# Wider pieces for the weight conversion, and the other head first in the products with v

## The chip, the cores and the metric

One core of one Trainium2 chip runs one program. The metric is device time in microseconds (us), from one execution to the next the same work; the profile that is read below is one more execution of the same program, taken with the hardware profiler. PE is TensorE, PEld its weight loads, DVE VectorE, ACT ScalarE, POOL GpSimd, SP the queue that issues the DMAs.

## The reference

Three blocks follow each other, for 4 batches of 576 tokens:

```python
# attention: 8 heads of 64, the 32 largest scores of each row are kept
scores = scale * (q @ k^T); mask = scores >= 32nd largest of the row
attn = softmax(scores where mask); x = attn @ v          # (4, 576, 512)
# gate: causal convolution over 5 tokens, two 512x512 products
x = (sigmoid(conv(x)) * (x @ w_val)) @ w_out
# phase mixer
theta = x @ w_theta
y = w_tok_r @ (x * cos(theta)) + w_tok_i @ (x * sin(theta))
u = x + y; out = u + max(u @ w_ch, 0)
```

The weights of the last two blocks arrive as float64 and have to be made float32 on the chip: `w_val`, `w_out`, `w_theta`, `w_ch` are 512x512, `w_tok` stands as 1152 rows of 576, `conv` as 512 rows of 5.

## The kernel before, in words

**Steps.** The attention works on 144 tiles of 128 rows of scores (576 wide), about one tile a step. Two heads (j = 0 and 1) of one pair share a part: a part's tiles are listed with head 0 first and head 1 last (lines 144 to 152). In step i several tiles are in flight: scores of tile i+3 on PE (`scores_pe`, line 530), their eviction on ACT, the largest values of tile i on DVE (`pick`, lines 581 to 587), a sign count on ACT (line 594), a product on POOL (`below`, lines 602 and 603), the threshold on DVE (`rest`, line 608), the exponential on ACT, the mask on DVE (`mask`, line 661), the transposes on PE (`turn`, line 674) and their eviction to `pT` on ACT (`turn_out`, line 693). The order of these stages in a step is the list `SOON`, in the second half of the steps `STEP` (lines 58 to 60, loop at line 1348). Lines 71 and 124 hold the engines DVE and ACT to the order in which the program is written; the order of PE, POOL and SP is chosen when the program is built, by what is ready.

**The end of a part.** When a part's last tile has been turned, `close` (line 708) issues the product with v, `px` (lines 760 to 766): for each of 5 blocks of keys one product for head 0, into partitions 0 to 63, and one for head 1, into partitions 64 to 127. There are 32 such groups, of 256 or 320 columns. Each product is two records in the profile, so a group has 20.

**Jobs.** The gate and the mixer of a batch are `front` and `back` (lines 840 and 1086): generators whose products are cut into portions that `work` (line 1224) puts into the steps, some 4150 ns of PE work a step (`BASE`), in the order of the batches. A job that meets something not yet written yields "sync" and tries again in the next step. `back` first waits until every weight is converted (`while any(lacking.values())`, line 1101).

**The conversion.** `weights` (line 358) cuts the six weights into pieces of 128 rows and `half` = 256 columns, 54 in all: 52 with 256 numbers a partition, one with 64 and one with 20. `convert` (line 1302) begins `PIECES` = 1 piece a step, and each piece moves on one stage a step through `cvt` (line 305):

1. a DMA brings the 64-bit words into one of six raw buffers (`RAWS`, line 53; line 318);
2. a step of waiting (`WAIT`), then on ACT the absolute value of the high words into one of two `tmp` buffers (line 329) and the shifted low words (line 330);
3. three DVE operations are put on the list `fill` (lines 337, 338 and 333): two of one input on `tmp`, one of two inputs;
4. `mask_between` (line 1275) takes three from `fill` in a step: the first, then the mask of line 661, then the second and third;
5. POOL adds the two words into the weight (line 351) and, for `w_theta`, ACT scales it (line 355); then `lacking` falls by one.

The raw and `tmp` buffers stand in memory that later holds the split halves of weight blocks (`hi0` to `hi3`, `lo0` to `lo3`, `place`, line 441). `want` (line 453) asks for the halves of block m of a weight as soon as the block before it is out (lines 867, 896, 1098 and 1148).

Of the kernel before, what the change touches and what calls it, by code (L numbers as in the profile page):

```python
# [12 lines left out]
F32R = mybir.dt.float32r  # L13
# [36 lines left out]
PARTS = (1, 1)  # L50
DRAIN = 5000.0
VAT = (11, 12)
RAWS = ("hi0", "hi1", "hi2", "hi3", "lo2", "lo3")
WAIT = 1
PIECES = lambda i: 1.0

LEAST = 2.0 ** -15 * 1.125
STEP = ['close', 'rest', 'below', 'pick', 'nmax', 'select', 'mask', 'check', 'expo', 'mid', 'chains', 'turn_out', 'convert', 'turn', 'scores_out', 'later', 'count', 'work_1', 'scores_pe', 'work_2', 'loads', 'chains']
# [32 lines left out]
def mixer(ctx, tc, qT, kT, vt, w_val, conv_t, w_out, w_theta, w_tok, w_ch, out, flag):  # L91
# [213 lines left out]
    def cvt(name, dst, words, factor, c):  # L305


        p0, a, w = dst.shape
        n = a * w
        r, k = c % len(W["raw"]), c % len(W["tmp"])  # L310
        while r in taken:
            yield None
        taken.add(r)
        raw = W["raw"][r][:p0, :n]
        t = W["tmp"][k][:p0, :n]
        lo, hi = raw[:, :, 0], raw[:, :, 1]
        def bring_in():
            ins = nc.sync.dma_start(raw.rearrange("p (a w) t -> p a w t", a=a), words).ins
            if c < len(RAWS):
                tc.add_manual_dep(ins, evicted[0].name, mybir.DependencyInfo(  # L320
                    mybir.DependencyClass.Sync, mybir.DependencyReason.SCHED_ONLY), reason="behind the heads")
            if loaded[0] is not None:
                tc.add_manual_dep(ins, loaded[0].name, mybir.DependencyInfo(
                    mybir.DependencyClass.NoSync, mybir.DependencyReason.SCHED_ONLY), reason="heads go first")

        yield bring_in

        def on_act():
            nc.scalar.activation(t, hi.bitcast(F32), AF.Abs)
            nc.scalar.activation(lo, lo.bitcast(U32), AF.Copy, scale=2.0 ** -29)  # L330

        def joined():
            nc.vector.scalar_tensor_tensor(hi, hi, -0x40000000, t.bitcast(I32), ALU.bitwise_and, ALU.bitwise_or)
            taken.remove(("tmp", k))

        def on_dve():
            fill.append(lambda: nc.vector.tensor_scalar(t, t, LEAST, None, ALU.max))
            fill.append(lambda: nc.vector.tensor_scalar(
                t.bitcast(I32), t.bitcast(I32), 3, 0x3FFFFFF8, ALU.logical_shift_left, ALU.bitwise_and))
            fill.append(joined)  # L340

        for _ in range(WAIT):
            yield None
        while ("tmp", k) in taken:
            yield None
        taken.add(("tmp", k))
        yield on_act
        yield on_dve
        while ("tmp", k) in taken:
            yield None  # L350
        yield lambda: nc.gpsimd.tensor_tensor(dst.bitcast(I32), *(h.rearrange("p (a w) -> p a w", a=a) for h in (hi, lo)),
                                                ALU.add)
        taken.remove(r)
        if factor is not None:
            yield lambda: nc.scalar.activation(dst, dst, AF.Copy, scale=factor)
        lacking[name] -= 1

    def weights():
        half = DM // 2
        W["raw"] = [ml.tile([P, half, 2], I32, tag=t, name=f"raw_{t}") for t in RAWS]  # L360
        W["tmp"] = [ml.tile([P, half], F32, tag=f"lo{x}", name=f"tmp{x}") for x in range(2)]
        pieces = []
        for name, src, factor in (("conv", conv_t, None), ("val", w_val, None), ("out", w_out, None),
                                  ("theta", w_theta, 1.0 / (2.0 * math.pi)), ("tok", w_tok, None), ("ch", w_ch, None)):
            rows, n = src.shape
            W[name] = cp.tile([P, -(-rows // P), n], F32, tag=f"w_{name}", name=f"w_{name}")
            words = src.bitcast(I32).rearrange("r (n t) -> r n t", t=2)

            chunks = -(-rows // P)
            cuts = [(c, 1, o, o + half) for c in range(chunks) for o in range(0, n - half + 1, half)]  # L370
            cuts += [(c, min(4, chunks - c), n // half * half, n) for c in range(0, chunks, 4) if n % half]
            for c, a, o, e in cuts:
                src = words[c * P : (c + a) * P, o:e].rearrange("(a p) n t -> p a n t", a=a)
                lacking[name] = lacking.get(name, 0) + 1
                pieces.append((name, W[name][:, c : c + a, o:e], src, factor, len(pieces)))
        return pieces
# [64 lines left out]
    def place(k, m):  # L441

        if k < 3 or k % 3 == 2:
            return [ml.tile([P, DM], F32R if k < 3 else I32, tag=f"{t}{m}", name=f"{t}{m}_{k}") for t in ("hi", "lo")]
        if (k, 0) not in places:
            names = ("val", "out") if k % 3 == 0 else ("theta", "ch")
            for t in range(2):
                places[k, t] = cp.tile([P, NC, DM], I32, tag=f"w_{names[t]}", name=f"w{t}_{k}")
        return [places[k, t][:, m, :] for t in range(2)]
# [3 lines left out]
    def want(b, name, last=NC - 1):  # L453

        k = PHASES.index((b, name)) if b else -1
        if k > 2:
            return
        for m in range(last + 1):
            if (b, name, m) in mats:
                continue  # L460
            src = W[name][:, m, :] if name == "theta" else W[name][:, :, m * P : (m + 1) * P]
            both = place(k, m)
            mats[b, name, m] = both
            stored[name, m] = dp.tile([P, 2, DM], I32, name=f"{name}{m}")

            def store(both=both, to=stored[name, m]):
                for t in range(2):
                    nc.sync.dma_start(to[:, t, :], both[t].bitcast(I32))

            hi, lo = (t if name == "theta" else t.rearrange("p (c w) -> p c w", c=NC) for t in both)  # L470
            halve(hi, lo, src, ("w", b, name, m), store)
# [236 lines left out]
    def close(part):  # L708
# [50 lines left out]
        owed[0] -= 8.3 * w  # L759
        px = ps_m.tile([P, w], F32, tag="m", name=f"px_{u}_{x}")  # L760
        for c in range(NF + 1):
            for j in range(2):
                d = slice(64 * j, 64 * j + 64)
                of_v, k = (v[:, c, d], j * NF + c) if c < NF else (v_last[:, d], 2 * NF)
                nc.tensor.matmul(px[d, :], of_v, pT[:, k, :],  # L765
                                 start=(c == 0), stop=(c == NF), skip_group_check=True)
# [73 lines left out]
    def front(b, xs):  # L840
# [13 lines left out]
        def val_out(m, x, ps):  # L854
            lo, hi = COLS[x]

            def f():
                g = gv[m][:, lo:hi]
                nc.vector.scalar_tensor_tensor(g, g, 1.0, ps, ALU.add, ALU.mult)
                if not three:  # L860
                    done.add(("G", b, m, x))
                    return
                if m == NC - 1:
                    for c in range(NC):
                        halve(*chunk(b, x, "G", c), gv[c][:, lo:hi], ("G", b, c, x))
                if x:
                    want(b, "out", m)
            return f

# [20 lines left out]
        def x2_out(m, x, ps):  # L890
            lo, hi = COLS[x]

            def f():
                nc.scalar.activation(x2T[:, m, lo:hi], ps, AF.Copy, scale=0.5)
                if three and x:
                    want(b, "theta", m)
                if three and m == NC - 1:
                    halve_room(b, x, "L", x2T)
                done.add(("x2", b, m, x))
            return f  # L900
# [185 lines left out]
    def back(b):  # L1086
        x2T = ms.pop(b)

        def y_out(m, h, ps):
            lo, hi = COLS[h]  # L1090

            def f():
                nc.vector.tensor_tensor(x2T[:, m, lo:hi], ps, x2T[:, m, lo:hi], ALU.add)
                if m == NC - 1 and (h or b == B - 1):
                    for k in (h,) if b == B - 1 else range(2):
                        halve_room(b, k, "U", x2T)
                if not h:
                    want(b, "ch", m)
            return f

# [40 lines left out]
        def h_out(m, h, ps):  # L1141
            lo, hi = COLS[h]

            def f():
                nc.vector.scalar_tensor_tensor(x2T[:, m, lo:hi], ps, 0.0, x2T[:, m, lo:hi], ALU.max, ALU.add)
                n = b + 1
                if h and n in THREE:
                    want(n, "val", m)
                    if (n * NP + m, 0) in there:
                        split_x(n, m, 0)  # L1150
                done.add(("o", b, m, h))
            return f
# [121 lines left out]

    def mask_between(i):

        for x in range(3):
            if fill:
                fill.pop(0)()
            if x == 0:  # L1280
                inside(i, mask)
# [122 lines left out]
```

## Time and profile before

| | |
|---|---|
| median of 3 runs | 838.05 us (836.03 to 838.68) |
| the profiled execution's own time | 838.7 us |
| its span, first to last instruction | 836.9 us |
| PE busy | 734.5 us, 88% |
| DVE busy | 677.7 us, 81% |
| ACT busy | 639.4 us, 76% |
| POOL busy | 440.5 us, 53% |
| mean granted TensorE clock | 0.969 of full |

The attention's tiles and the jobs run side by side for some 700 us; after that only jobs are left. A busy share is a mean over stages with different limits, so the time is cut into windows first. The records of one engine overlap a little at their ends (the next instruction starts before the last has finished), so the cost of an operation on an engine that never idles is read from start to start.

### The profile page before, as it was taken

The page shows a single profiled execution, that of the slowest core. Times are in us where ns is not written, and L with a number is a line of the kernel's source. Part 1 is how long each engine was busy: PE and PEld are TensorE (multiplying, and loading weights), DVE is VectorE, ACT ScalarE, POOL GpSimd, SP SyncE. Part 2 cuts the span into 40 slices and gives each one's busy share as a digit, 9 for nine tenths or more (in the row PEclk, how much of TensorE's full clock was granted, in tenths as well). Part 3 has the DMA queues.
Part 4 walks back from the last instruction along what each step waited for, and adds up shares of the span by engine and source line. Part 5 has one row for each costly group of instructions (what it writes and reads, how often), then busy time and mean ns, then how long its engine had stood idle before and what let it go on. Part 6 is the DMA issues. An engine that isn't in the chain of part 4 may idle for free.

```text
span 836.9 us, 15761 instructions
## 1 busy us (share of the span) xinstructions
PE 734.5 (88%) x4478; PEld 584.1 (70%) x4478; DVE 677.7 (81%) x2786; ACT 639.4 (76%) x1573; POOL 440.5 (53%) x583
## 2 busy tenths in 40 slices
PE   4476889968899899898699989999989899999995
PEld 3244667535665676697587777778988767898895
DVE  6999999979987889999899879989998685353522
ACT  6678898889788777989789888889987785346511
POOL 5876665545643536557677735547796143004600
PEclk9999899979999899999899989999999999999998
DMA  5566666635440253437455543234753300070002
GB/s 167 147 159 194 165 171 168 179 94 129 119 108 15 47 156 82 101 93 224 112 179 168 151 138 84 45 84 112 193 166 119 101 1 15 1 231 28 2 1 61
DMA packets 73601, 94.35 MB, mean 113 GB/s; under 512 B 13728, under 2 KB 37152, under 8 KB 73504
## 3 DMA queue, kind: packets, MB, share of 16 engines
q1 hardware_dynamic: 73184, 92.82, 40.8%
q8 instruction: 38, 0.62, 0.3%
q10 hardware_dynamic: 320, 0.43, 0.2%
q14 instruction: 59, 0.48, 0.2%
HBM read 49.96 MB, written 13.11 MB: 75 GB/s over the span
## 4 chain that ended last, share of the span: by engine, by line
PE 39%; DVE 32%; ACT 13%; POOL 6%; issue 5%; DMA 4%; SPq 0%; ACTq 0%; POOLq 0%
PE py L1114 8%; DVE cand L581 7%; DVE thrs L608 5%; PE px L765 5%; DVE s L661 4%; PE pth L516 4%; PE ph L516 3%; PE px2t L516 3%; PE pval L516 3%; PE py L1133 3%; DVE cand L587 3%; DVE tops L585 3%; PE pt L674 3%; ACT n L594 2%; POOL y L602 2%
## 5 line engine op out<-in xcount | busy, mean ns | idle before, releaser
L602 POOL TENSOR_TENSOR y<-s,n 128x576 f32<-128x576 f32 x144 | 190.9, 1325 | 158.1 <-DVE thrs L608 116.0
L581 DVE MAX8 cand<-s 128x8 f32<-128x96 f32 x864 | 211.4, 245 | 1.0 <-ACT s L559 1.0
L661 DVE SCALAR_TENSOR_TENSOR s<-s,thrs,e 128x576 f32<-128x576 f32 x144 | 137.7, 956 | 9.7 <-ACT e L202 9.7
L594 ACT ACTIVATE n<-s,tops 128x576 bf16<-128x576 f32 x144 | 112.1, 779 | 40.3 <-POOL y L602 18.8
L559 ACT ACTIVATE s<-ps 128x256 f32<-128x256 f32 (+1 forms) x288 | 103.1, 406 | 26.2 <-PE ps L737 10.3
L1114 PE MATMUL py<-w_tok,z 128*128 128x256 f32 (+1 forms) x432 | 118.8, 416 | 1.7 <-DVE z L973 1.7
L674 PE MATMUL pt<-ident,s 128*128 128x128 f32 x576 | 95.3, 286 | 28.4 <-ACT pT L693 15.4
L608 DVE MAX8 thrs<-y 128x8 f32<-128x584 f32 x144 | 109.5, 760 | 8.3 <-POOL y L603 8.0
L202 ACT ACTIVATE e<-s,least 128x576 f32<-128x576 f32 x144 | 110.9, 770 | 0.5 <-DVE s L661 0.4
L674 PEld LDWEIGHTS pt<-ident,s 128*128 128x128 f32 x576 | 69.0, 145 | 56.5 <-ACT pT L693 25.9
L545 PE MATMUL ps<-kh_None,q 128*128 128x256 f32 x240 | 92.0, 390 | 5.2 <-ACT rb L744 2.5
L1114 PEld LDWEIGHTS py<-w_tok,z 128*128 128x128 f32 x432 | 79.6, 195 | 22.3 <-DVE z L973 2.5
L765 PE MATMUL px<-pT,v 128*64 128x256 f32 (+1 forms) x512 | 84.5, 431 | 10.1 <-ACT pT L693 10.1
L693 ACT COPY pT<-pt 128x512 f32<-128x512 f32 x128 | 73.2, 572 | 24.4 <-PE pt L674 13.4
L585 DVE MAX8 tops<-cand 128x8 f32<-128x48 f32 x432 | 83.3, 193 | 0.1
L546 PE MATMUL ps<-kl_None,q 128*128 128x256 f32 x240 | 71.5, 301 | 0.0
L765 PEld LDWEIGHTS px<-pT,v 128*64 128x64 f32 x512 | 37.1, 141 | 43.4 <-issue 12.5
L545 PEld LDWEIGHTS ps<-kh_None,q 128*128 128x128 f32 x240 | 46.7, 195 | 20.2 <-ACT s L559 8.3
L545 PE MATMUL ps<-kh,q 128*128 128x256 f32 (+1 forms) x80 | 35.7, 454 | 24.3 <-ACT s L559 11.0
L587 DVE MATCH_REPLACE8 cand<-tops,cand 128x48 f32<-128x48 f32 x288 | 55.5, 193 | 0.0
L546 PEld LDWEIGHTS ps<-kl_None,q 128*128 128x128 f32 x240 | 47.1, 196 | 2.3 <-issue 0.9
L682 ACT COPY pT<-ps 64x128 f32<-64x128 f32 (+1 forms) x160 | 39.4, 246 | 12.0 <-PE ps L678 5.6
(215 smaller groups left out, 1742.2 us busy)
## 6 DMA issues: line engine op xcount, KB each, us to landing
kh_None<-kh_None SPq DMA_DIRECT2D x48, 144.0 KB, 2.6
kl_None<-kl_None SPq DMA_DIRECT2D x48, 144.0 KB, 2.7
v<-in_vt_dram SPq DMA_DIRECT2D x20, 256.0 KB, 3.4
out_dram<-x2T SPq DMA_DIRECT2D x16, 256.0 KB, 3.4
w<-ch SPq DMA_DIRECT2D x16, 256.0 KB, 4.1
w<-theta SPq DMA_DIRECT2D x16, 256.0 KB, 5.6
raw_hi<-in_w_tok_dram SPq DMA_DIRECT2D x14, 256.0 KB, 4.1
kh<-kh SPq DMA_DIRECT2D x24, 144.0 KB, 2.5
```

What stands on the lines that cost most here:

```text
L202: ins = nc.scalar.activation(out, src, func, **more).ins
L516: nc.tensor.matmul(ps[o : o + n], x, y, start=(i + k == 0), stop=(i == last and k == len(ways) - 1), skip_group_check=(n < P))
L545: nc.tensor.matmul(bank[:, :w], q2, kh[:, lo:hi], start=(j == js[0]), stop=False)
L546: nc.tensor.matmul(bank[:, :w], q2, kl[:, lo:hi], start=False, stop=(j == js[-1]))
L581: nc.vector.max(d["cand"][:, k, 8 * x : 8 * x + 8], s_tiles[i][:, x * SUB : (x + 1) * SUB])
L594: nc.scalar.activation(n, s_tiles[i], AF.Sign, bias=d["tops"][:, k, KC - 1 : KC], scale=-(1.0 + 2.0 ** -22), accum_out=acc)
L602: nc.gpsimd.tensor_tensor(y[:, :S], s_tiles[i], d.pop(("n", k)), ALU.mult)
L608: nc.vector.max(thrs[:, N - 1 - i : N - 1 - i + NK], d.pop(("y", k)))
L661: nc.vector.scalar_tensor_tensor(p, p, thr(i), e.exp, ALU.is_ge, ALU.mult, accum_out=part["sums"][:, e.slot : e.slot + 1])
L674: nc.tensor.transpose(e.pt[:, c, :], p[:, c * P : (c + 1) * P], ident)
L765: nc.tensor.matmul(px[d, :], of_v, pT[:, k, :], start=(c == 0), stop=(c == NF), skip_group_check=True)
L1114: nc.tensor.matmul(ps, z[:, m * P : (m + 1) * P], W["tok"][:, w, lo:hi], start=(i + k == 0), stop=(i == NF))
```

## The change

Pieces are 512 columns wide, so there are 28: 26 with 512 numbers a partition (one of them 8 strips of 64 columns of `w_tok`), one with 64 and one with 20. One begins every other step. The raw buffers are three of double size, `tmp` two of double size. The second ACT operation (line 330) moves one step later, and two operations instead of three are taken from `fill` in a step, so that they fall: first, mask, second; in the next step: third, mask. The halves of weight blocks stand in pairs of blocks, and `want` asks for them two at a time. In `px` head 1's product goes before head 0's.

```diff
-RAWS = ("hi0", "hi1", "hi2", "hi3", "lo2", "lo3")
+RAWS = ("hi01", "hi23", "lo23")
 WAIT = 1
-PIECES = lambda i: 1.0
+PIECES = lambda i: 0.5
...
-        def on_act():
+        def size():
             nc.scalar.activation(t, hi.bitcast(F32), AF.Abs)
+
+        def tail():
             nc.scalar.activation(lo, lo.bitcast(U32), AF.Copy, scale=2.0 ** -29)
...
         def on_dve():
+            tail()
             fill.append(lambda: nc.vector.tensor_scalar(t, t, LEAST, None, ALU.max))
...
-        yield on_act
+        yield size
         yield on_dve
...
     def weights():
-        half = DM // 2
+        half = DM
...
-            cuts += [(c, min(4, chunks - c), n // half * half, n) for c in range(0, chunks, 4) if n % half]
+            cuts += [(c, min(8, chunks - c), n // half * half, n) for c in range(0, chunks, 8) if n % half]
...
     def place(k, m):
 
         if k < 3 or k % 3 == 2:
-            return [ml.tile([P, DM], F32R if k < 3 else I32, tag=f"{t}{m}", name=f"{t}{m}_{k}") for t in ("hi", "lo")]
+            dt = F32R if k < 3 else I32
+            both = []
+            for t in ("hi", "lo"):
+                if (t, m) in (("lo", 0), ("lo", 1)):
+                    both.append(ml.tile([P, DM], dt, tag=f"{t}{m}", name=f"{t}{m}_{k}"))
+                    continue
+                pair = f"{t}{m - m % 2}{m - m % 2 + 1}"
+                if (pair, k) not in places:
+                    places[pair, k] = ml.tile([P, 2, DM], dt, tag=pair, name=f"{pair}_{k}")
+                both.append(places[pair, k][:, m % 2, :])
+            return both
...
         for c in range(NF + 1):
-            for j in range(2):
+            for j in (1, 0):
                 d = slice(64 * j, 64 * j + 64)
...
-                if x:
+                if x and m % 2:
                     want(b, "out", m)
...
-                if three and x:
+                if three and x and m % 2:
                     want(b, "theta", m)
...
-                if not h:
+                if not h and m % 2:
                     want(b, "ch", m)
...
                 if h and n in THREE:
-                    want(n, "val", m)
+                    if m % 2:
+                        want(n, "val", m)
...
-        for x in range(3):
+        for x in range(2):
             if fill:
                 fill.pop(0)()
```

## Rows read from the trace of the kernel before

**Rows 1.** Windows: span, busy us of each engine (records), clock, DMA share, GB/s.
```profile
40.00:60.00 20.00, 14.90 (x57) 9.17 (x57) 19.86 (x93) 15.44 (x41) 14.09 (x20) 1.00 0.60 158
...
120.00:140.00 20.00, 19.61 (x112) 15.06 (x111) 19.86 (x93) 17.65 (x50) 12.84 (x18) 1.00 0.70 178
...
200.00:220.00 20.00, 16.06 (x87) 11.19 (x87) 19.86 (x93) 19.28 (x52) 12.51 (x17) 0.91 0.52 142
...
280.00:300.00 20.00, 20.00 (x111) 14.99 (x111) 17.79 (x76) 14.32 (x38) 8.85 (x11) 1.00 0.31 80
```

**Rows 2.** Timeline of DVE, 69.7 to 74 us: start, length, then the operation.
```profile
69.74 0.28 DVE L337 TENSOR_SCALAR tmp<-tmp 128x256 f32<-128x256 f32 x1
69.93 0.81 DVE L661 SCALAR_TENSOR_TENSOR s<-s,thrs,e 128x576 f32<-128x576 f32 x1
...
70.67 0.29 DVE L338 TENSOR_SCALAR tmp<-tmp 128x256 int32<-128x256 int32 x1
71.00 0.43 DVE L333 SCALAR_TENSOR_TENSOR raw_lo<-raw_lo,tmp 128x256 int32<-128x256 int32 x1
...
73.66 0.28 DVE L337 TENSOR_SCALAR tmp<-tmp 128x256 f32<-128x256 f32 x1
```

**Rows 3.** DVE by line, 40 to 120 us: count, busy us, mean ns of one.
```profile
L338 DVE TENSOR_SCALAR tmp<-tmp 128x256 int32<-128x256 int32 x18 | 7.4, 413 | 0.0
```

**Rows 4.** Line 338 in the whole run: ns least/median/most, forms; the chain of waits.
```profile
L338 DVE TENSOR_SCALAR tmp<-tmp x54: 191/289/1480, 18.9 to 276.4; 128x256 int32<-128x256 int32 x52, 128x20 int32<-128x20 int32 x1, 128x64 int32<-128x64 int32 x1
...
277.12 2.39 DVE z L973 x4
```

**Rows 5.** Timelines of DVE and POOL at 71 and at 81 us.
```profile
71.56 0.61 POOL L351 TENSOR_TENSOR w_out<-raw_lo 128x256 int32<-128x256 int32 x1 [1.44 <-ACT e L202]
...
81.47 1.57 POOL L253 TENSOR_TENSOR kl<-kl,kh 128x576 fp32r<-128x576 f32 x1
...
81.68 1.97 DVE L661 SCALAR_TENSOR_TENSOR s<-s,thrs,e 128x576 f32<-128x576 f32 x1
```

**Rows 6.** Timelines of PE around four groups of products with v.
```profile
45.84 1.12 PE L765 MATMUL px<-pT,v 128*64 128x256 f32 x2
...
288.13 0.65 PE L765 MATMUL px<-pT,v 128*64 128x256 f32 x2
288.70 1.56 PE L1114 MATMUL py<-w_tok,z 128*128 128x256 f32 x6
290.19 0.65 PE L765 MATMUL px<-pT,v 128*64 128x256 f32 x4
290.78 0.39 PE L545 MATMUL ps<-kh_None,q 128*128 128x256 f32 x1
...
291.62 1.29 PE L765 MATMUL px<-pT,v 128*64 128x256 f32 x9
...
293.49 0.66 PE L674 MATMUL pt<-ident,s 128*128 128x128 f32 x4
...
369.92 1.95 PE L765 MATMUL px<-pT,v 128*64 128x256 f32 x16
...
372.23 0.33 PE L674 MATMUL pt<-ident,s 128*128 128x128 f32 x1
...
676.14 0.65 PE L765 MATMUL px<-pT,v 128*64 128x256 f32 x2
```

**Rows 7.** Line 351's last additions; the timeline of PE at 408 us.
```profile
L351 POOL TENSOR_TENSOR w_ch<-raw_lo x4: 612/612/615, 235.3 to 277.2; 128x256 int32<-128x256 int32 x4
...
408.39 0.63 PE L516 MATMUL pval<-X,hi 128*128 128x320 f32 x1 [4.90 <-DVE gp L859]
```

**Rows 8.** ACT by line and form: count, busy us, mean ns; line 318's DMAs.
```profile
L329 ACT ACTIVATE tmp<-raw_hi 128x256 f32<-128x256 f32 x34 | 15.0, 442 | 1.4 <-DVE raw_lo L333 1.4
...
L930 ACT ACTIVATE gp<-pth,magic 128x512 f32<-128x512 f32 x14 | 9.5, 684 | 3.3 <-PE pth L516 3.2
...
DMA to landing us min/median/max: 2.5/3.6/5.9
```

## The prediction

> **What bounds the kernel now.** I read the windows first. In the stretch of the conversion DVE is full and PE is not: from 40 to 60 us DVE is busy 19.86 of 20 us and PE 14.90, and the three windows up to 120 us look alike; from 200 to 220 us again DVE 19.86, PE 16.06 [rows 1]. From 120 to 140 us PE is nearly full too (19.61), and from 280 to 300 us PE is full (20.00) and DVE no longer (17.79) [rows 1]. So work taken from DVE counts up to 120 us and from 200 to 220 us, and work taken from PE counts around 130 us and from 280 us on.
>
> Then the timeline of DVE at 70 us: one step, from one line 337 to the next, takes 73.66 - 69.74 = 3.92 us without a gap, and the conversion's three operations are in it [rows 2]. Last the timeline of PE around the products with v: some groups stand in one piece, others are cut up by foreign products [rows 6].
>
> **The conversion on DVE.** From start to start a piece of 256 columns costs 69.93 - 69.74 = 0.19, 71.00 - 70.67 = 0.33 and 71.34 - 71.00 = 0.34 us (line 333 ends what it shares of the engine as line 608 starts, 0.09 us before its own record's end at 71.43), together 0.86 [rows 2]. Two such pieces cost 1.72. For 512 columns: line 333 has two inputs, and four such operations of 512 columns take 2.39 us, 0.60 each [rows 4]. Line 338 took 191 ns with 20 columns and 289 with 256, so 98 / 236 = 0.42 ns a column and 0.11 us for 256 more [rows 4]; I give line 337 the same. So 0.30 + 0.44 + 0.60 = 1.34, a saving of 0.38 a pair, 0.19 for each old piece. Two things come on top. Line 333 now follows line 338 at once and starts when its record of 0.29 has ended, where line 661 starts 0.09 us before line 337's end [rows 2]; in the new order line 333 stands a step later, which frees some 0.13 a pair. And line 338 has a mean of 413 ns in this stretch against a median of 289 [rows 3, 4]: 0.12 us of waiting, which with half as many operations is met half as often, 0.06 for an old piece. Together 0.19 + 0.06 + 0.06 = 0.31; I take 0.28, as some waits will move to the mask.
>
> Eighteen pieces lie between 40 and 120 us [rows 3]; at the same pace four more lie from 200 to 220 us. 22 x 0.28 = **6.2 us less**. The other 30 lie beside a full PE or ACT, or where everything waits for the start: 0, at most 30 x 0.28 = 8.4.
>
> **The conversion on ACT, POOL and SP.** On ACT one operation of 512 columns takes 684 ns, two of 256 take 884 [rows 8]: 0.2 less for each of two operations a pair. ACT isn't what DVE waits for, so nothing, but it keeps ACT from becoming the bound (it is busy 19.28 of 20 at 200 us [rows 1]). POOL's addition grows from 0.61 to at most 1.22 us every other step [rows 5]; it runs while DVE does other things: 0 (its meeting with the mask is a rival). SP issues 28 loads instead of 54. A load of 256 columns lands in 2.5 to 5.9 us, median 3.6 [rows 8]; twice the bytes take from 3.6 to 11.8, I take 7.2. The absolute value comes two steps behind the load, 2 x 3.92 = 7.8 us [rows 2]: hidden. If it weren't, ACT would stand in its order before the load, with the evictions of scores behind it, up to 4.0 us each time. With three raw buffers the next load waits for the addition of one step before, not two; behind it on SP stand the loads of heads and v, which are issued several steps ahead.
>
> **The port of POOL and DVE.** The mask (line 661) takes 0.81 us [rows 2], but 1.97 where POOL's line 253 had started 0.21 us earlier and ran for 1.57 [rows 5]. In the old order the addition started at 71.56, 0.13 us after line 333's record ended at 71.43, and met line 608, which has one input; in the new order the mask follows line 333 directly. It starts before line 333's record ends, so before POOL can be released: it is first, and the addition waits. The Trainium skill's page "SBUF — State Buffer", section "SBUF: two separate sides", says that a two-input DVE operation and a POOL operation that reads this memory hold one shared port in turn, whoever starts first for its whole length. The row of 1.97 us agrees; the page doesn't say who is first here.
>
> **The order of the products with v.** Twelve of the 32 groups begin with a lone pair of records, from the one at 45.84 to the one at 676.14 us [rows 6]: head 0's first product, ready before head 1's column, since head 1's tiles are turned last. At 288 us the pieces take 288.70 - 288.13 = 0.57, 290.78 - 290.19 = 0.59 and 293.49 - 291.62 = 1.87, together 3.03 us; a whole group takes 372.23 - 369.92 = 2.31 [rows 6]. A broken group costs 0.72 us of PE. With head 1 first, nothing of the group is ready before its last column, and after it everything is, so I expect whole groups. Where PE is full that is time: one broken group around 130 us, two between 280 and 300 us, and one later in a stretch like that: 4 x 0.72 = **2.9 us less**. Bounds: 0, and 12 x 0.72 = 8.6.
>
> **The weights are ready later.** Before, piece k begins in step k and its addition is written four steps on: the last (k = 53) in step 57, and `lacking` falls in step 58. After, piece k begins in step 2k + 1 and its addition is written five steps on, as its third DVE operation needs a second step: the last (k = 27) in step 60, `lacking` falls in 61. Before, the last addition ran at 277.2 us [rows 7]. So `back` of batch 0 can start three steps later, some 3 x 4.4 = 13 us (18 pieces, one a step, in 80 us [rows 3]). I price it at 0: after batch 0's work, the gate's products of batch 1 wait for the attention anyway (PE stands 4.90 us before 408.39 until DVE has written gp [rows 7]), so the delay ends in that wait, and the three steps without jobs are short ones. Without that cover it costs up to 13.
>
> **The pairs of blocks.** For four matrices (w_ch of batch 0, three of batch 1) the halves of an even block are asked for one block later, and a pair's memory is free when both blocks are. The last block's time doesn't move, and the products that need it wait for it today: 0. At worst one step of 3.92 [rows 2] for each, 16.
>
> **Sum.** -6.2 - 2.9 = -9.1 us on the profiled execution's 838.7, so 829.6; the median of the runs shown is 0.65 lower: **829.0 us**.
>
> **Rivals.** *The products stay broken* (the change of order doesn't do what I read into it): another product can be ready while px isn't complete, and breaks are seen in the middle of groups too (291.62 after 290.19 [rows 6]). Only the conversion counts: 838.05 - 6.2 = 831.9. Chance 0.19.
>
> *DVE's time turns into waiting for something else.* ACT is at 19.28 of 20 in one of the two stretches [rows 1]; against it, ACT is relieved as well, and is at 15.44 in the other. Then only PE's part counts, and part of that: 838.05 - 2.9 = 835.2 to no change. Chance 0.17.
>
> *The addition gets ahead of the mask.* Place: every second step, between line 333 and line 661. Price: up to 1.97 - 0.81 = 1.16 us [rows 2, 5] for each of the 11 wide pieces in DVE's full stretches, 12.8; it decides if POOL is released before the mask starts. 829.0 + 12.8 = 841.8, **slower**. Against it: the mask starts before line 333 has ended, as above. Chance 0.08.
>
> *The later weights are not covered.* 829.0 + 13 = 842, chance 0.06.
>
> **The numbers.** My forecast has 0.50. What a measurement of this kernel can tell from no change is about 0.3%, 2.5 us, so faster means below 835.5 and slower above 840.6. Faster: 0.50 + 0.19 + about a third of the third case, 0.05: 0.74. Same: the rest of the third case, 0.12, and 0.01 from the edges of the last two: 0.13. Slower: 0.13. Range: downwards the forecast with all of the conversion's 8.4 more gives 820.6, and some of the broken groups beyond four go with it: 820; upwards it takes in the third case: 838. The other cases, and the far ends for the loads and the pairs, are the 2 in 10 left out.
>
> **What would show it.** Lines 337, 338 and 333 with 26 records of 512 columns near 0.4, 0.4 and 0.69 us; from 40 to 120 us about 19 or more tiles instead of 18 and DVE still full; groups of px of 20 records in one piece; the mask's records of 0.81 as before next to an addition of 1.1 to 1.2; `py` of batch 0 about three steps later than before, and the first `px2t` of batch 1 at the same tile as before. It is wrong if the masks grow behind line 351, if DVE gains idle time up to 120 us, or if the jobs of batch 1 start later by as much as those of batch 0.

## The result, and the profile after

The kernel after takes 829.74 us (median of 5 runs, 828.74 to 832.65), beside 838.23 us (5 runs, 836.03 to 839.63): ratio 0.9908, interval 0.9894 to 0.9923: faster by the forecast's own bound of 835.5 us. Forecast were 829.0 us, 820 to 838, faster with 0.74. Measured a second time beside other runs of the kernel before (839.04), it took 832.41 us, ratio 0.9924 (0.9894 to 0.9954).

The profiled execution of after took 829.74 us, its span 827.9. Lines of after stand 2 to 13 further down than those of before: 337, 338 and 333 are 340, 341 and 335, the addition 351 is 354, the mask 661 is 674, the products with v 765 are 778, `py` 1114 is 1127. The page's busy times of after:

```profile
PE 725.3 (88%) x4478; PEld 584.6 (71%) x4478; DVE 669.0 (81%) x2708; ACT 634.0 (77%) x1517; POOL 451.7 (55%) x557
```

DVE is 8.7 us less busy and PE 9.2, POOL 11.2 more. The windows of [rows 1] again, and the one from 260 us (columns as there):

```profile
40.00:60.00 20.00, 13.11 (x67) 9.59 (x66) 19.18 (x84) 16.65 (x40) 16.61 (x18) 0.95 0.72 184
120.00:140.00 20.00, 19.99 (x118) 15.93 (x116) 19.86 (x90) 17.90 (x45) 13.05 (x16) 1.00 0.61 163
200.00:220.00 20.00, 19.72 (x107) 15.49 (x106) 18.43 (x78) 16.30 (x42) 12.88 (x18) 1.00 0.50 133
260.00:280.00 20.00, 9.31 (x32) 5.76 (x32) 16.60 (x50) 16.21 (x37) 9.52 (x11) 0.50 0.22 48
280.00:300.00 20.00, 20.00 (x122) 15.68 (x121) 16.33 (x84) 14.66 (x37) 10.28 (x13) 0.92 0.35 88
```

Early on DVE still sets the pace (from 40 to 120 us it is busy 78.6 of 80 us, 79.4 before). From 200 to 220 us PE has taken over, and from 260 to 280 us PE is busy less than half of the time, at a granted clock of 0.50 (1.2 GHz), and full right after it. Behind that stretch after loses a part of what it has won, as the next table shows.

One pair of pieces in after's timeline of DVE, then POOL's addition of that pair (start, length, operation):

```profile
89.13 0.41 DVE L340 TENSOR_SCALAR tmp<-tmp 128x512 f32<-128x512 f32 x1
89.46 0.81 DVE L674 SCALAR_TENSOR_TENSOR s<-s,thrs,e 128x576 f32<-128x576 f32 x1
...
90.19 0.42 DVE L341 TENSOR_SCALAR tmp<-tmp 128x512 int32<-128x512 int32 x1
90.53 0.76 DVE L621 MAX8 thrs<-y 128x8 f32<-128x584 f32 x1
...
92.85 0.67 DVE L335 SCALAR_TENSOR_TENSOR raw_lo<-raw_lo,tmp 128x512 int32<-128x512 int32 x1
93.44 0.81 DVE L674 SCALAR_TENSOR_TENSOR s<-s,thrs,e 128x576 f32<-128x576 f32 x1
```

```profile
93.66 1.49 POOL L354 TENSOR_TENSOR w_out<-raw_lo 128x512 int32<-128x512 int32 x1 [0.78 <-DMA v_last<-in_vt_dram]
```

From start to start a clean pair costs 0.33 + 0.34 + 0.59 = 1.26 us; 1.34 were forecast. The mask behind line 335 keeps its 0.81 us, and the addition, which starts 0.22 us after it, has a record of 1.49.

**The lead.** To see where time is won and lost, I take the start of the mask's record of a tile from each kernel's timeline of DVE and subtract that of before. In us (minus is ahead of before), single profiled executions; the last two columns are the start of batch 0's first `py` on PE, and `py`'s busy time on PE up to the mask of tile 54:

| tile | 0 | 24 | 51 | 54 | 57 | 60 | 72 | span | `py` from | `py` to 54 |
|---|---|---|---|---|---|---|---|---|---|---|
| before, start | 29.5 | 135.5 | 275.6 | 291.5 | 305.3 | 317.1 | 372.2 | 836.9 | 268.0 | 11.1 |
| after | -3.6 | -8.1 | -12.3 | -9.6 | -12.3 | -8.1 | -7.2 | -9.0 | 286.3 | 0 |
| after_again | -3.6 | -8.3 | -12.5 | -9.8 | -12.1 | -8.0 | -7.0 | -8.4 | 286.4 | 0 |
| split_dve | -3.7 | -2.9 | -5.5 | -2.5 | -4.9 | -0.8 | +0.2 | +1.2 | 293.6 | 0 |
| late_start | -3.6 | -2.6 | -2.9 | -0.6 | -2.6 | -1.1 | -1.3 | -1.6 | 275.8 | 9.9 |
| px_alone | -0.3 | +0.1 | -0.8 | -0.8 | -0.8 | -0.8 | +0.3 | -2.3 | 267.3 | 9.8 |
| gate_later | -0.2 | -0.2 | -0.4 | -0.7 | -4.6 | -1.8 | -3.7 | -0.9 | 278.1 | 8.8 |
| conv_alone | -3.8 | -8.4 | -11.7 | -9.0 | -12.9 | -11.5 | -12.3 | -12.8 | 266.9 | 9.4 |
| gate_tok | -3.4 | -7.8 | -11.8 | -8.7 | -11.2 | -10.2 | -7.6 | -9.7 | 256.3 | 5.5 |
| gate_tok_px0 | -3.5 | -6.9 | -10.2 | -7.1 | -11.0 | -10.4 | -9.7 | -8.1 | 258.0 | 10.5 |
| no_last_dve | -3.6 | -7.7 | -11.6 | -12.0 | -12.5 | -8.3 | -7.3 | -4.3 | 284.5 | 0 |
| ends_early | -3.4 | -7.0 | -10.6 | -7.9 | -9.7 | -5.6 | -4.6 | -3.3 | 288.9 | 0 |
| early_tok | -3.8 | -8.3 | -13.2 | -10.2 | -13.3 | -12.2 | -9.6 | -11.1 | 254.9 | 6.1 |
| slow_fast | -3.6 | -8.5 | -14.4 | -11.4 | -13.9 | -14.1 | -16.4 | -16.0 | 290.5 | 0 |

In after the lead is 12.3 us at tile 51, where the sum had 6.9 (the conversion's 6.2 and one group's 0.72), and 8.1 nine tiles later. How far one execution can be trusted: after_again is the same kernel as after, and in ends_early and early_tok every engine's instructions come in the order of after and of gate_tok. Between such executions a lead differs by up to 2.6 us at tile 72, and by 5.7 in the span, but the fall from tile 57 to 60 repeats within 0.1. The spans of split_dve, no_last_dve and ends_early are of executions some 3 us above their medians, that of conv_alone of one 3 us below.

### The profile page after: what moved, and what is told of

Its sections match the earlier page's. It is cut to its first block, busy times and chain, and to the rows that moved or that the text cites. A ratio compares the mean times of both kernels' runs of the same rounds, so it can differ in the third digit from the quotient of the medians.

```text
span 827.9 us, 15411 instructions
## 1 busy us (share of the span) xinstructions
PE 725.3 (88%) x4478; PEld 584.6 (71%) x4478; DVE 669.0 (81%) x2708; ACT 634.0 (77%) x1517; POOL 451.7 (55%) x557
## 4 chain that ended last, share of the span: by engine, by line
PE 47%; DVE 27%; ACT 15%; POOL 4%; issue 3%; DMA 2%; SPq 1%; ACTq 0%; POOLq 0%; DVEq 0%
PE py L1127 9%; PE px L778 8%; DVE cand L594 5%; PE ph L529 4%; DVE s L674 4%; DVE thrs L621 4%; PE px2t L529 4%; PE pval L529 4%; PE pth L529 4%; PE pt L687 3%; PE py L1146 3%; PE ps L558 3%; ACT n L607 2%; DVE cand L600 2%; DVE gp L843 2%
## 5 line engine op out<-in xcount | busy, mean ns | idle before, releaser
L615 POOL TENSOR_TENSOR y<-s,n 128x576 f32<-128x576 f32 x144 | 188.9, 1312 | 205.0 <-DVE thrs L621 144.0
L572 ACT ACTIVATE s<-ps 128x256 f32<-128x256 f32 (+1 forms) x288 | 103.7, 406 | 33.5 <-PE ps L691 11.5
L1127 PE MATMUL py<-w_tok,z 128*128 128x256 f32 (+1 forms) x432 | 115.0, 407 | 3.4 <-DVE z L986 3.4
L558 PE MATMUL ps<-kh_None,q 128*128 128x256 f32 x240 | 93.7, 397 | 5.9 <-ACT s L572 3.9
L1127 PEld LDWEIGHTS py<-w_tok,z 128*128 128x128 f32 x432 | 77.8, 190 | 22.3 <-DVE z L986 5.0
L778 PE MATMUL px<-pT,v 128*64 128x256 f32 (+1 forms) x512 | 75.3, 430 | 17.3 <-ACT pT L706 17.3
L778 PEld LDWEIGHTS px<-pT,v 128*64 128x64 f32 x512 | 34.1, 142 | 47.2 <-ACT pT L706 19.7
L695 ACT COPY pT<-ps 64x128 f32<-64x128 f32 (+1 forms) x160 | 39.2, 245 | 11.5 <-PE ps L691 5.6
```

Source lines behind the costliest of these rows:

```text
L558: nc.tensor.matmul(bank[:, :w], q2, kh[:, lo:hi], start=(j == js[0]), stop=False)
L615: nc.gpsimd.tensor_tensor(y[:, :S], s_tiles[i], d.pop(("n", k)), ALU.mult)
L778: nc.tensor.matmul(px[d, :], of_v, pT[:, k, :], start=(c == 0), stop=(c == NF), skip_group_check=True)
L1127: nc.tensor.matmul(ps, z[:, m * P : (m + 1) * P], W["tok"][:, w, lo:hi], start=(i + k == 0), stop=(i == NF))
```

## The experiments

Each ratio is to runs of the kernel before taken alongside on the same chip (medians 838.8 to 839.0 us).

**px_alone.** Only the products' order.

```diff
-            for j in range(2):
+            for j in (1, 0):
```

> The kernel before with one edit: head 1's product goes before head 0's in the products with v. As forecast, four broken groups in stretches with a full PE become whole, 0.72 us each: 2.9 us less, ratio about 0.9965, and no px group begins with a lone pair of records. Rival: in the trace of after the lone pairs are gone, but twelve groups are still cut in two by a product of the scores, so a group saves less or the time saved is waited for elsewhere: between 1 us less and no change, ratio 0.999 to 1.000.

835.32 us, ratio 0.9958 (0.9942 to 0.9973): 3.5 us less, between 2.3 and 4.9. The forecast's term holds in size. One of the four groups, in px_alone's timeline of PE:

```profile
505.91 0.65 PE L765 MATMUL px<-pT,v 128*64 128x256 f32 x4
506.49 0.39 PE L545 MATMUL ps<-kh_None,q 128*128 128x256 f32 x1
...
507.33 1.52 PE L765 MATMUL px<-pT,v 128*64 128x256 f32 x12
508.68 0.60 PE L765 MATMUL px<-pT,v_last 128*64 128x256 f32 x4
509.21 0.66 PE L674 MATMUL pt<-ident,s 128*128 128x128 f32 x4
```

The lone pair is gone, but a product of the scores still cuts the group: (506.49 - 505.91) + (509.21 - 507.33) = 2.46 us; before's group there took 3.04 by the same reading, and the one of the forecast 3.03 [rows 6]. So a group saves some 0.58 rather than 0.72. Its places hold in part: the lead in this trace grows by 1.1 us behind the group of 505 us and by 0.8 behind that of 676, and not between 280 and 300 us (0.8 from tile 51 to 60), where PE now stands 1.34 us before a group, for ACT's line 693.

**conv_alone.** After with `for j in range(2)` again.

> The kernel after with head 0's product first again: pieces of 512 columns, pairs of blocks and the later weights alone. As forecast: 838.2 - 6.2 = 832.0 us, ratio 0.9926, the first mask at the time of before and the gain spread over 40 to 120 us. Rival: nearly the whole gain of after is here (829.5 to 830.5 us, ratio 0.990 to 0.991), 3.6 us of it before the first mask, since the products' order brings next to nothing.

828.85 us, ratio 0.9886 (0.9868 to 0.9904): 9.6 us less. The rest of the change gives all the gain by itself; with the 3.5 us of px_alone, after would have to be 13 us faster than before, and it is 7.7. The two gains do not add up. The first masks are as early as in after, so the rival's picture of the start holds too, but not its reason: the order of the products is worth something alone.

**gate_later.** In before, three steps pass before the last piece counts as converted.

```diff
+        for _ in range(3 * (c == 53)):
+            yield None
         lacking[name] -= 1
```

> The kernel before with one edit: after the last of the 54 pieces three steps pass before the weights count as converted, so that back of batch 0 starts three steps later, as in the kernel after, and nothing else changes. As forecast: no change, within 0.5 us, as the delay ends in a wait that the gate's products of batch 1 have anyway. Rival: slower by about 4 us, ratio 1.004 to 1.006, since in the trace of after the lead over before falls from 12.3 us at tile 51 to 8 us at tile 72, behind a gap of PE between 256 and 279 us. Far end: 13 us, ratio 1.016.

837.95 us, ratio 0.9981 (0.9969 to 0.9993). Not slower, if anything 0.6 to 2.6 us faster: in the kernel before, the delay is covered, as forecast. But the edit moves `py` by 10.1 us only, from 268.0 to 278.1, and 8.8 us of its work are done by the mask of tile 54; in after it starts 18.3 us later than in before.

**gate_tok.** After, with `back` of batch 0 waiting for `w_tok` alone before its first block of `py`, and for `w_ch` before the others (m > 0). So one of eight blocks, 18 records, is let go early.

```diff
-        while any(lacking.values()):
+        while lacking["tok"]:
             yield "sync"
...
+                while m and lacking["ch"]:
+                    yield "sync"
                 yield from after(*[("z", b, i) for i in SETS[0]])
```

> The kernel after with a looser gate: back of batch 0 waits for w_tok alone, and for w_ch from its second block on, so it is no longer held back by the later weights. If the delay costs nothing, as forecast, the time stays at after's 829.7 us (ratio 0.990). If the delay costs about 4 us, they come back: about 826 us, ratio 0.985, the lead of 12 us over before at tile 51 is kept to the end, and the gap of PE around 256 to 279 us is no longer than the 6.2 us of before.

828.11 us, ratio 0.9862 (0.9845 to 0.9880), clear of after's interval: 11.6 us less than before instead of 7.7. So in after the late gate does cost something, some 4 us, though it costs nothing in before. The lead does not stay at 12: it is 10.2 at tile 60 and 7.6 at tile 72, so the trace shows 2.1 us of the gain at tile 60 and nearly none at 72. `py` in the windows of three kernels (span, PE busy with it, clock, DMA share, GB/s), first after:

```profile
260.00:280.00 20.00, 0.00 (x0) 0.50 0.22 48
280.00:300.00 20.00, 8.27 (x36) 0.92 0.35 88
300.00:320.00 20.00, 13.75 (x56) 1.00 0.36 100
```

Then gate_tok:

```profile
260.00:280.00 20.00, 3.56 (x10) 0.69 0.22 47
```

And conv_alone:

```profile
260.00:280.00 20.00, 9.42 (x34) 0.76 0.22 47
280.00:300.00 20.00, 4.38 (x18) 1.00 0.37 88
```

From 256 to 280 us PE has little to do, as ACT and then DVE are busy with the mixer's sine. PE in after at the start of this gap:

```profile
255.70 0.31 PE L559 MATMUL ps<-kl_None,q 128*128 128x320 f32 x1
263.86 0.48 PE L687 MATMUL pt<-ident,s 128*128 128x128 f32 x1 [7.85 <-ACT pT L706]
```

And in conv_alone:

```profile
264.42 1.11 PE L687 MATMUL pt<-ident,s 128*128 128x128 f32 x4 [7.26 <-ACT pT L706]
...
266.93 1.48 PE L1127 MATMUL py<-w_tok,z 128*128 128x256 f32 x3
```

The first 7 us stand idle in both. Then, in conv_alone, `py` fills the stretch up to 280 us; in after it starts at 286.3 us, when the gap is over. Both kernels seem to write it at the same step (the order of the instructions on DVE and on ACT is the same in the two traces): the order on PE is settled when the program is built.

**after_again** is the kernel after, unchanged, beside the next three; its result stands above.

> The kernel after, unchanged, beside the kernel before on the chip of the other runs of this call, so that it can be compared with them: ratio 0.9908 as before, 0.989 to 0.992.

**split_dve.** After, each wide DVE operation issued as two of 256 columns (`cols` holds the two halves).

```diff
-            nc.vector.scalar_tensor_tensor(hi, hi, -0x40000000, ...)
+            for z in cols:
+                nc.vector.scalar_tensor_tensor(hi[:, z], hi[:, z], -0x40000000, ...)
...
-            fill.append(lambda: nc.vector.tensor_scalar(t, t, LEAST, None, ALU.max))
+            fill.append(lambda: [nc.vector.tensor_scalar(t[:, z], t[:, z], LEAST, None, ALU.max) for z in cols])
```

> The kernel after with one edit: each of the conversion's three DVE operations is issued as two operations of 256 columns, while DMAs, ACT, POOL, the steps, the start and the gates stay as they are. By the forecast's working the wider operations save 0.38 us a pair by themselves and up to 0.56 with the waits met half as often; on the 11 pairs of the stretches with a full DVE this gives 4.2 to 6.2 us back: ratio 0.996 to 0.998. Rival, from the trace of after: much of the gain is the later start (3.6 us) and masks that wait less for POOL (2.6 us), which this edit leaves; then it gives back 2 to 3 us: ratio 0.993 to 0.995, and the first mask stays at 25.9 us.

836.72 us, ratio 0.9960 (0.9944 to 0.9975). It gives back 4.4 us beside after's first measurement (0.9960 - 0.9908) and 3.0 beside the second: by the first the forecast's 4.2 to 6.2 at its lower edge, by the second, where the intervals overlap, the rival's upper edge. The trace tells more. DVE by line over 11 pairs (count, busy us, mean ns), after from 36 to 128 us:

```profile
L674 DVE SCALAR_TENSOR_TENSOR s<-s,thrs,e 128x576 f32<-128x576 f32 x23 | 20.5, 891 | 0.8 <-ACT e L202 0.8
L341 DVE TENSOR_SCALAR tmp<-tmp 128x512 int32<-128x512 int32 x11 | 6.5, 589 | 0.0
L335 DVE SCALAR_TENSOR_TENSOR raw_hi<-raw_hi,tmp 128x512 int32<-128x512 int32 x7 | 5.7, 819 | 0.0
L340 DVE TENSOR_SCALAR tmp<-tmp 128x512 f32<-128x512 f32 x11 | 4.8, 436 | 0.0
L335 DVE SCALAR_TENSOR_TENSOR raw_lo<-raw_lo,tmp 128x512 int32<-128x512 int32 x4 | 3.3, 820 | 0.0
```

And split_dve (36 to 132 us):

```profile
L676 DVE SCALAR_TENSOR_TENSOR s<-s,thrs,e 128x576 f32<-128x576 f32 x22 | 18.5, 843 | 0.0
L343 DVE TENSOR_SCALAR tmp<-tmp 128x256 int32<-128x256 int32 x22 | 8.2, 411 | 0.0
L337 DVE SCALAR_TENSOR_TENSOR raw_hi<-raw_hi,tmp 128x256 int32<-128x256 int32 x15 | 7.3, 525 | 0.0
L342 DVE TENSOR_SCALAR tmp<-tmp 128x256 f32<-128x256 f32 x22 | 7.0, 360 | 0.0
L337 DVE SCALAR_TENSOR_TENSOR raw_lo<-raw_lo,tmp 128x256 int32<-128x256 int32 x8 | 3.5, 483 | 0.0
```

The conversion's records are 20.3 us in after and 26.0 in split_dve, 0.52 us a pair. And before, from 40 to 136 us:

```profile
L661 DVE SCALAR_TENSOR_TENSOR s<-s,thrs,e 128x576 f32<-128x576 f32 x22 | 22.6, 1027 | 0.0
L338 DVE TENSOR_SCALAR tmp<-tmp 128x256 int32<-128x256 int32 x21 | 8.3, 395 | 0.0
L337 DVE TENSOR_SCALAR tmp<-tmp 128x256 f32<-128x256 f32 x22 | 6.6, 302 | 0.0
L333 DVE SCALAR_TENSOR_TENSOR raw_hi<-raw_hi,tmp 128x256 int32<-128x256 int32 x14 | 6.0, 428 | 0.5
L333 DVE SCALAR_TENSOR_TENSOR raw_lo<-raw_lo,tmp 128x256 int32<-128x256 int32 x8 | 3.4, 427 | 0.3
```

Here the conversion's records are 24.3 us, so beside before the wide operations save 4.0 us, 0.36 a pair, and split_dve's narrow ones cost 1.7 more than before's own: not all that split_dve gives back is the width. The masks are shorter than before in both, a mean of 891 and 843 ns against 1027, some 3 us over 22 masks in after. That holds in this stretch only; over the whole run the mean is 956 ns before and 957 after.

**late_start.** Before, with the conversion begun two steps later.

```diff
-PIECES = lambda i: 1.0
+PIECES = lambda i: 1.0 if i > 1 else 0.0
```

> The kernel before with one edit: the conversion begins two steps later (its last piece and the gate of back with it). As forecast, with the start priced at 0: no change. Rival, from the trace of after, where the first mask came 3.6 us earlier: the first mask at about 26 us instead of 29.5, and this lead stays, 2.5 to 3.6 us less, ratio 0.996 to 0.997; the conversion's operations that left the start run at its end, beside a full PE.

837.90 us, ratio 0.9989 (0.9977 to 1.0002). That is 0.9 us less, between 1.9 less and 0.2 more. The first mask is 3.6 us earlier, as in after, and 2.9 of it are still there at tile 51; then the lead is 0.6 at tile 54, 2.6 at 57 and 1.1 at 60: most of what is saved at the start comes back around the end of the conversion. The forecast's 0 holds for the total, the rival for the first 275 us only.

**gate_tok_px0.** The kernel gate_tok with head 0's product first.

> The kernel gate_tok (after, with back of batch 0 waiting for w_tok alone) with head 0's product first again. If the gain of the products' order is real beside the conversion's and was lost in after only by the place of py, this is 2.5 to 3.5 us slower than gate_tok: ratio 0.989 to 0.991. If the two gains don't add up, it is as fast as gate_tok: ratio 0.985 to 0.987.

829.35 us, ratio 0.9881 (0.9861 to 0.9900). It lies 1.6 us above gate_tok, with overlapping intervals: inconclusive on the order of the products. But it tells something of the gate: conv_alone, the same kernel with the late gate, stands at 0.9886. With head 0 first the looser gate brings nothing, with head 1 first some 4 us.

**ends_early** and **early_tok.** After and gate_tok with more pieces from step 24 on.

```diff
-PIECES = lambda i: 0.5
+PIECES = lambda i: 0.5 if i < 24 else 0.6
```

> The kernel after with one edit: from step 24 on 0.6 pieces begin in a step instead of 0.5, so that the last begins in step 50 instead of 55 and the weights count as converted some two steps earlier than in the kernel before. Theory: in after, late_start and split_dve the lead over before falls by 2.3 to 3.0 us between tiles 51 and 54, as the last wide pieces run where DVE is full behind the mixer's sine (264 to 290 us); with the pieces gone from there the fall is under 1 us, py begins in the gap of PE, and the time is 2.5 to 5 us below after's: ratio 0.985 to 0.988. Rival, as the forecast had it: the place of the last pieces and the gate cost nothing, and the ratio stays at 0.990 to 0.992.

> Both edits together: the kernel after with 0.6 pieces a step from step 24 on, and back of batch 0 waiting for w_tok alone. If the gate of back is what counts, as fast as gate_tok or faster: ratio 0.983 to 0.986. If the place of the last pieces is what counts, as fast as ends_early.

832.30 us, ratio 0.9912 (0.9888 to 0.9936), and 829.08 us, ratio 0.9885 (0.9867 to 0.9904). The edit didn't do what it was meant to: ends_early's last line 335 starts at 283.07 us, 281.4 in after, and by every tile as many pieces are done as in after, so the pieces did not go faster; with three raw buffers, each held from the load to the addition, they probably can't. So it says nothing of the last pieces' place. The two are repeats of after and gate_tok. After has then been measured at 0.9908, 0.9924 and 0.9912, and gate_tok at 0.9862 and 0.9885. As a pair the two runs point the same way as the first (0.0027 of the time, 2.3 us), with overlapping intervals: the looser gate is worth some 2 to 5 us.

**slow_fast.** After with fewer pieces at first.

```diff
-PIECES = lambda i: 0.5
+PIECES = lambda i: 0.4 if i < 22 else 0.6
```

> The kernel after with 0.4 pieces a step up to step 22 and 0.6 from there on: the last begins in step 53 instead of 55. About two pairs fewer fall into the first stretch with a full DVE, 1.6 to 1.7 us each by the trace of after, and run from 200 us on, where DVE has idle time: the lead at tile 24 is about 11 us instead of 8. By the theory that what leaves this stretch is gained: ratio 0.985 to 0.988. Rival, as in late_start, where 2.5 us of lead from the start were lost again by tile 60: they come back as work beside the end of the conversion, ratio 0.990 to 0.991.

824.39 us (822.67 to 825.18), ratio 0.9826 (0.9809 to 0.9843): 14.6 us less than before, **faster than both kernels**. The edit does the first half of what it was meant to. Two pieces fewer than in after are done at tile 24, but the pieces never go faster than in after: 12 are done between tiles 24 and 48 in both, and the last line 335 starts at 296.65 us, in tile 59, against 281.38 and tile 54 in after. The reason is not the expected one either: at tile 24 the lead is 8.5 us, not 11, and the difference comes later. The window from 160 us, slow_fast:

```profile
160.00:180.00 20.00, 16.47 (x88) 10.51 (x87) 18.93 (x76) 19.32 (x44) 13.09 (x16) 0.93 0.45 115
```

And after:

```profile
160.00:180.00 20.00, 11.02 (x64) 6.94 (x62) 15.52 (x63) 17.17 (x36) 9.62 (x11) 0.74 0.35 92
```

PE is busy 5.4 us more there, at a higher clock. That fewer pieces are ready by then and batch 0's mixer comes at another tile is what differs; which of these fills the stretch was not tried. So the fastest kernel of all is the one whose weights are ready last and whose `py` starts at 290.5 us.

**no_last_dve.** After without the DVE operations of the last two pieces.

```diff
+            if c >= 26:
+                fill.extend([lambda: None, lambda: None, joined])
+                return
```

> The kernel after, but the three DVE operations of the last two pieces (half of w_ch) are left out, so that half of w_ch is not rounded right; their loads, ACT and POOL work, steps and gates stay. Theory: these six operations stand in the chain that DVE sets behind the mixer's sine, so the lead over before, which falls from 12.3 us at tile 51 to 9.6 at tile 54 in after, falls by under 1 us, and the time is 2 to 3 us less than after's: ratio 0.986 to 0.989. Rival, as the forecast had it: what lies behind the first stretch with a full DVE costs nothing, and the fall at tile 54 is 2.5 us or more all the same; ratio 0.990 to 0.992. Third case: the fall at tile 54 goes, but the lead at tile 75 is the same 8 us, since PE has the delayed products of back to make up; ratio 0.990 to 0.992.

831.68 us, ratio 0.9910 (0.9891 to 0.9929): the third case. In after's chain of waits these operations stand between 262 and 275 us (start, length, what):

```profile
264.19 0.34 DVE tmp L341
264.53 2.39 DVE z L986 x4
...
269.24 1.70 DVE raw_lo L335
270.94 0.74 DVE s L674 x2
271.68 1.51 DVE gp L843
```

And in that of no_last_dve:

```profile
264.85 2.40 DVE z L990 x4
...
269.56 1.70 DVE s L678 x2
271.26 0.74 DVE gp L847
```

Line 341 and line 335 are gone from the chain (the wait of a second behind POOL has moved to the mask), and the lead no longer falls at tile 54: 11.6, then 12.0. Yet at tile 60 it is 8.3 and at tile 72 7.3, as in after. What is gained on DVE there is lost within the next six tiles, where PE has `py` to make up. So the last pieces cost nothing that the total shows (0.9910, beside 0.9908 to 0.9924 for after).

## Why the prediction was right, point by point

The number is right, the sum behind it only in part: the lead at tile 51 is larger than the terms gave, and a step that was priced at 0 took some 2 to 5 us back. That the two nearly cancel, and the total meets the forecast to 0.7 us, is luck.

**The conversion on DVE: the size of its term holds up to tile 51, not to the end.** Up to tile 51 the width is worth 12.3 - 5.5 = 6.8 us (after against split_dve; 5.1 with the lead of ends_early), 6.2 forecast, and a part of that is split_dve's own cost; over the whole run it is 3.0 to 4.4. Clean durations are as worked out (1.26 us a pair for 1.34; medians of 408, 422 and 674 ns in the rows of lines 340, 341 and 335, near 0.4, 0.4 and 0.69). Not foreseen was the size of the lead: of the other 5.5 us at tile 51, 2.9 are the later start (late_start), 0.8 the products' order (px_alone, no more than executions of one kernel differ by), and the rest, 1.8, is left for masks that wait less. That is what remains, it was not tried by itself; in the rows above the masks of after are 3 us shorter.

**The start, priced at 0:** right in the total, where late_start's interval takes in no change.

**The port.** The mask is first and the addition waits, as the forecast had it: the median of the mask in the whole run is 806 ns, and there is no sign of the rival in which the addition gets ahead. "At most 1.22 us" for the addition holds for its work and not for its record. One wide addition in after had no mask beside it:

```profile
78.89 1.03 POOL L354 TENSOR_TENSOR w_out<-raw_hi 128x512 int32<-128x512 int32 x1
```

Nearly all others show 1.48 to 1.55 us, so about 0.45 of a record is waiting. In the timeline above, 0.59 of the 1.49 us from 93.66 on lie beside the mask, whose record ends at 94.25. The Trainium skill's page "SBUF — State Buffer", section "SBUF: two separate sides", says that of a two-input DVE operation and a POOL operation that reads this memory the one that starts first has the shared port for its whole length. The trace agrees: the mask's record starts 0.22 us earlier and keeps its 0.81 us, and the addition's is longer.

**The loads.** 512 columns land in 1.8 to 6.0 us, median 4.0, where I took 7.2; hidden all the same.

**The products' order: right alone, not beside the rest.** px_alone gives 3.5 us where 2.9 were forecast. In after, 12 of the 32 groups are still cut in two, none begins with a lone pair, and its lead grows by 1.1 us behind the group that before has at 505 us and by 0.8 behind that of 676. But conv_alone is no slower than after.

**"The weights are ready later: I price it at 0" is the step that failed, in the kernel with both changes.** Its reason, that the delay ends in a wait of batch 1's gate products, looks at the jobs alone. By that sign it came true: the first `px2t` of batch 1 comes in tile 85 in both kernels. But `py` of batch 0 comes in tile 56 instead of 51, five tiles later and not three, and the loss falls on the attention's own tiles, long before batch 1's gate: in after 0 us of `py` are done by tile 54, instead of 11.1; PE then stands at 1.2 GHz, has 22 us of `py` to do from 280 to 320 us beside the tiles, and the lead falls from 12.3 to 8.1 us between tiles 57 and 60. The same fall of 4.1 to 4.2 us stands in split_dve, ends_early and no_last_dve, all without `py` before tile 54; with 5 to 10 us of it done (gate_tok, early_tok, gate_tok_px0, conv_alone, late_start, px_alone) it is 0 to 1.5, but 2.8 in gate_later with 8.8 done. slow_fast is the exception: its weights are ready latest, no `py` is done before tile 54, and there is no fall. So lateness alone has no fixed price: it costs nothing in before (gate_later) nor with head 0 first (conv_alone against gate_tok_px0), some 2 to 5 us in after (gate_tok), and slow_fast wins in spite of it. The rival "the later weights are not covered" had the place where the cost begins; its 13 us were too much and its sign didn't decide, since the lead was larger.

**What stays open:** why the build puts `py` behind the gap with one order of the products and into it with the other. What the late `py` costs is about what the order gains, and this is the likely reason that the gains do not add up; that is argued from the traces, and `py` was not moved by itself with everything else kept. Nor do the traces of gate_tok and early_tok show the whole gain in one place: at tile 72 their leads are 7.6 and 9.6 us, after's in three executions 7.2, 7.0 and 4.6.

## What to carry to other kernels

Follow the lead tile by tile, not the total: a change can win 12 us, lose 4 and look like the 8 that were forecast. Take it from two executions of one kernel first, to know how far it repeats. Work that is held back by a gate is free only if the gap that it used to fill is filled by something else; price the gap, not only the wait behind it. And where a conversion runs beside other work, its pace (here 0.4 pieces a step at first, 7 us less than after by the ratios) may be worth as much as the width of its operations.

## What was not expected of the hardware

A record on POOL includes its wait for DVE: nearly all wide additions show 1.48 to 1.55 us, the one above that met no mask 1.03, and one of 256 columns that met nothing 0.61 [rows 5]. Operations of one input wait as well, not only the mask. In after's timelines of DVE and of POOL:

```profile
39.91 1.63 DVE L341 TENSOR_SCALAR tmp<-tmp 128x512 int32<-128x512 int32 x1
```

```profile
39.33 1.93 POOL L253 TENSOR_TENSOR kl<-kl,kh 128x576 fp32r<-128x576 f32 x1
```

POOL's operation ends at 41.26 us and line 341, 0.42 us long in the median, at 41.54. And twice the bytes in one load cost little: 4.0 us to landing instead of 3.6 [rows 8].
